# Shen attention and a SwiGLU block on one core: the opening list merged into the first chunk, w_out loaded in two halves, weight sums in two parts, and new orders for every chunk

## Chip, cores, metric

One core of a Trainium2 chip. The metric is the device time of one execution in microseconds. The kernel before was run 13 times: median 299.17 us, lowest 298.19, highest 301.69.

## What is computed

Eight batches of eight heads, 576 positions, head size 64. The attention is a linear one, and its output is the input of a gated block:

```
q_s = softmax of q over the head dimension
k_s = softmax of k over the positions
kv  = einsum('bhsd,bhse->bhde', k_s, v)
x   = einsum('bhsd,bhde->bhse', q_s, kv), rearranged to 4608 tokens x 512
out = (silu(x @ w_gate) * (x @ w_val)) @ w_out      # 512 -> 1536 -> 512
```

## The kernel before

**Attention of a batch** is done for two groups of heads, G = 0 and 1. `load` (line 80) brings q, k or v of a group with one DMA from SyncE's queue into the pool `ld` (three buffers for q, two for k and two for v). `exp` (126) is one ScalarE activation over 128 x 1152. `cast_v` (133) turns v into bf16 in one of two fixed tiles, one per group. `norm_sum` (140) and `norm_mul` (149) normalise q. The normalised q is transposed, by TensorE with a copy out of PSUM (`tr`, 158; for batches 0 and 1) or by a DMA (`tr_dma`, 177; later batches). `kv` (186) and `kn` (206) form the 64 x 64 matrices, `x` (229) or `x_pair` (260) multiply by them, and copies put the result as 16-bit columns into the ring `xt`.

**The gated block** takes the first 576 tokens by plain products: `First` (300), whose step I is one 128-column block of x @ w_gate with its silu, and J the same block of x @ w_val with the product with the silu. `Unit` (470) multiplies 128 of these tokens by w_out in two steps of six matmuls of 512 columns. All other tokens go by a seven-product scheme on 2 x 2 blocks: `Pair` (359) for the first two matrices, steps a b c d e f g and v; `Quad` (510) for w_out, steps A to H; a sixth block pair goes by plain products, `Direct` (434), steps G and U. The scheme needs sums of weight quarters, `g_sum` (333, four of them, in `gt`) and `w_sum` (488, four, in `wt`), sums of x columns (`x_sum`, 342) and of hidden columns (`h_sum`, 494).

**The order of the work** is written out by hand. `tc.manual_schedule()` keeps the order of the program on every engine. A plan is a string of tokens, which `chunk` (746) hands to `op` (673) one by one: `I3`, `a0`, `S042` and so on are the steps above with their block; `eq0:1` is the exp of q of group 0 of batch 1, `ek` that of k, `cv` the cast of v, `ns`, `nd` and `nm` the sums and products of the softmax, `tr` the transposed copy, `kk` and `kv` the kv products, `xz` and `xx` the x products, `Q`, `W`, `X`, `Y`, `S`, `T` the sums, `pe` and `silu` a one-column activation that brings the table of exp or silu, `load` the loads of the batch after. A star sends an evicting or elementwise step to the other of two engines. So each engine works through its own instructions in plan order, and a step that waits holds back everything after it on its engine.

There are five plans: PLAN_B (first 576 tokens and batch 1's attention), PLAN_0 (448 tokens), PLAN for chunks 1 to 5, PLAN_N for 6 and 7, and PLAN_E for the last w_out products.

**Loads and waits.** Weights are cast to fp16 by DMAs from GpSimd's queue (`w_slice`, 98; `wo_slice`, 106). Before the plans the program issues seven for w_gate and w_val, `w_dma[0]` to `[6]`, and three of four row blocks for w_out, `w_dma[7]` to `[9]`. An explicit dependency holds w_dma[7] back until w_dma[5] has landed, batch 1's q until w_dma[4] has, batch 1's first k until w_dma[8] has, and the second k until w_dma[9] has (lines 632 to 669). PSUM is one pool of eight banks (line 60); each I or J step takes two of them, until ScalarE or VectorE has emptied them.

Of the kernel before, what the change touches and what calls it, by code (L numbers as in the profile page):

```python
# [12 lines left out]
SYNC = mybir.DependencyInfo(mybir.DependencyClass.Sync, mybir.DependencyReason.DATA)  # L13
# [3 lines left out]
def kernel(  # L17
# [19 lines left out]
    nc = tc.nc  # L37

    B, H, S, D = q.shape
# [11 lines left out]
    NP = 5  # L51
# [15 lines left out]
    wo = const.tile([128, MT, d_model], FP16, name="wo", tag="wo")  # L67
# [9 lines left out]
    dmas = {}  # L77
    raw = {}

    def load(b, G, what, src, after=None):  # L80
        raw[what, b, G] = ld.tile(
            [128, 2, T * 64], FP32, tag=what, name=what, bufs=3 if what == "q" else None
        )
        ap = bass.AP(
            tensor=src.tensor,
            offset=src[b, 4 * G].offset,
            ap=[[T * 64, 128], [2 * HSTR, 2], [1, T * 64]],
        )
        d = nc.sync.dma_start(out=raw[what, b, G], in_=ap)
        if after is not None:  # L90
            tc.add_manual_dep(d.ins, after.ins.name, SYNC, reason="order of loads")
        dmas[what, b, G] = d

    def load_group(b, G):
        for what, src in (("q", q), ("k", k), ("v", v)):
            load(b, G, what, src)
# [9 lines left out]
    def wo_slice(m0, n):  # L106
        ap = bass.AP(
            tensor=moe_w_out.tensor,
            offset=moe_w_out[m0 * 128, 0].offset,
            ap=[[d_model, 128], [128 * d_model, n], [1, d_model]],  # L110
        )
        return nc.gpsimd.dma_start(out=wo[:, m0:m0 + n, :], in_=ap)
# [9 lines left out]
    A, Z = BANKS = ((0, 5), (5, 9))  # L122
# [10 lines left out]
    def cast_v(b, G, eng, t0=0, t1=T):  # L133
        copy(
            eng,
            vbs[G][:, t0:t1, 0:128].rearrange("p t (h d) -> p t h d", d=64),
            raw["v", b, G].rearrange("p h (t d) -> p t h d", d=64)[:, t0:t1],
        )
# [38 lines left out]
    def tr_dma(b, G):  # L177
        s = st[b, G]
        qt = at.tile([128, T, 2, 64], BF16, tag="qtd", name="qtd")
        nc.sync.dma_start_transpose(  # L180
            out=qt.rearrange("p t g c -> p t (g c)"),
            in_=s["qs"].rearrange("p t c -> p (t c)"),
        )
        s["qt"] = [qt[:, :, g, :] for g in range(2)]
# [417 lines left out]
    with tc.manual_schedule():  # L602
# [29 lines left out]
        tc.add_manual_dep(w_dma[0].ins, dmas["k", 0, 0].ins.name, SYNC, reason="order of loads")  # L632
        load(1, 0, "q", q, after=w_dma[4])
        load(1, 1, "q", q)
        for m0 in (0, 4, 8):
            w_dma.append(wo_slice(m0, 4))
        tc.add_manual_dep(w_dma[7].ins, w_dma[5].ins.name, SYNC, reason="order of loads")

        warm_up(WARM[0])
        for G in range(NG):  # L640
# [17 lines left out]
        x(0, 1, A)  # L658
        x(0, 1, Z)

        load(1, 0, "k", k, after=w_dma[8])
        load(1, 0, "v", v)
        load(1, 1, "k", k, after=w_dma[9])
        load(1, 1, "v", v)
        load(2, 0, "q", q, after=dmas["k", 1, 0])
        load(2, 0, "k", k, after=dmas["v", 1, 0])
        load(2, 0, "v", v, after=dmas["k", 1, 1])
        load(2, 1, "q", q, after=dmas["v", 1, 1])
        load(2, 1, "k", k, after=dmas["q", 2, 0])

        n_ch = n_tok // 512 - 1

        def op(t, ci, c0, h, parts):
            alt = t.endswith("*")
            t = t.rstrip("*")
            t, b = t.split(":") if ":" in t else (t, ci + 2)
            b = int(b)
            k, a, nm = t[0], t[1:], t[:2]
            if nm in ATT:
                G = int(t[2]) if t[2:3].isdigit() else 0  # L680
                if b >= B or nm == "lo" and b + 1 >= B and ci >= 0:
                    return
                if nm == "eq":
                    exp(b, G, "q")
                elif nm == "ek":
                    exp(b, G, "k")
                elif nm in ("si", "pe"):
                    f = AF.Silu if nm == "si" else AF.Exp
                    nc.scalar.activation(out=warm, in_=zero[:, 0:1], func=f)
                elif nm == "cv":  # L690
                    cast_v(b, G, nc.vector if alt else nc.gpsimd)
                elif nm == "ns":
                    norm_sum(b, G)
                elif nm == "nm":
                    norm_mul(b, G, nc.vector if alt else nc.gpsimd)
                    tr_dma(b, G)
                elif nm == "lo":
                    if ci < 0:
                        load(b, 1, "v", v)
                    else:  # L700
                        load_group(b + 1, 0)
                        load_group(b + 1, 1)
                elif nm == "kv":
                    kv_pair(b)
                elif nm == "xx":
                    x_pair(b, nc.scalar if alt else nc.vector)
                elif nm == "nd":
                    norm_mul(b, G, nc.gpsimd if alt else nc.vector)
                elif nm == "tr":
                    tr(1, G, BANKS[int(t[3])], nc.vector)  # L710
                elif nm == "kk":
                    kv_kn(b, G, split=True)
                elif nm == "xz":
                    x(1, G, BANKS[int(t[3])], nc.scalar if alt else nc.vector)
            elif k in "abcdefgv":
                parts["p" + a].run(k, alt)
            elif k in "GU":
                parts["m" + a].run(k)
            elif k in "IJ":
                parts["i" + a].run(k)  # L720
            elif k == "O":
                parts["u" + a[0]].run(int(a[1]), alt)
            elif k in "ABCDEFH":
                parts["o"].run(k, alt)
            elif k in "SR":
                k0 = int(a[1])
                h_sum(ci + (k == "R"), int(a[0]), k0, k0 + int(a[2]))
            elif k == "X":
                if ci + 1 < n_ch:
                    x_sum(c0 + 2 * h, 256, int(a), nc.gpsimd if alt else nc.vector)  # L730
            elif k == "Y":
                x_sum(c0, h, int(a), nc.gpsimd if alt else nc.vector)
            elif k == "W":
                w_sum(int(a), nc.gpsimd if alt else nc.vector)
            elif k == "Q":
                g_sum(int(a), nc.vector if alt else nc.gpsimd)
            elif k == "T" and ci == B - 2:
                i = int(a)
                if i == 0:
                    parts["t"] = ld.tile(  # L740
                        [128, 4, 2, 2, 128 * (HM - NP)], FP16, tag="q", name="gt2", bufs=3
                    )
                gt2[i] = parts["t"][:, i]
                g_sum(i, nc.gpsimd if alt else nc.vector, 128 * NP, 128 * HM, gt2)
# [11 lines left out]
            for t in plan.split():  # L756
                op(t, ci, c0, n // 2, parts)

        ATT = ("pe", "eq", "ek", "si", "cv", "ns", "nm", "lo", "kv", "xx", "nd", "tr", "kk", "xz")
        ORDER = (0, 1, 2, 3, 4, 5)  # L760
        gt2 = [None] * 4
        PLAN_B = """
        I0 I1 pe:1 I2 I3 J0 J1 I4 I5 J2 J3 J4 Q0 I6 J5 I7 J6 J7 eq0:1 ns0:1 eq1:1 I8
        nd0:1* ns1:1 J8 I9 J9 I10 Q1* nd1:1* I11 cv0:1 tr00 J10 J11 tr10 ek0:1 O01 Q3*
        cv1:1 ek1:1 O11 tr01 kk0:1 O02 tr11 eq0:2 O12 kk1:1 ns0:2 O21 xz10* ek0:2 xz00*
        O22 Q2 xz01 eq1:2 cv0:2 xz11 O31 load:2 nm0:2 cv1:2 O32 ek1:2
"""
        PLAN_0 = """
        a0 ns1 G5 b0 G11 Y0 c0 Y2 Y1 v0 Y3* d0* W2 a1 f0 b1 U5 c1 g0 d1 W0 v1 e0 a2 f1 b2
        v2 kv silu:2 nm1 g1 d2 a3 e1 c2 f2 b3 c3 e2 g2 d3 v3 e3 a4 f3 xx* load g3 W1 d4*  # L770
        b4 c4* X0 f4 v4 U11 e4* X2* X1 W3 X3 g4*
"""
        PLAN = """
        a0 S042 b0 G5 c0 d0 A v0 S002 a1 f0 b1 S142 c1 v1 U5 S242 g0 pe S222 B S022 S102
        S122 S302 d1 S322 ek0 e0 a2 S342 e1 eq0 ns0 S202 C ek1 f1 D E eq1 cv1 b2 c2* silu
        F nm0 cv0 g1 d2 v2 ns1 a3 nm1 H* f2 kv g2 d3 b3 c3 v3 e2 load f3 e3 a4 b4 c4 g3 v4
        d4* e4 xx* f4 X2 G11 g4 X0 X1 X3* U11
"""
        PLAN_N = """
        a0 S222 b0 c0 d0 T0* A v0 S002 f0 a1 e0* S042 b1 g0 d1 c1 S022 v1 a2 f1 S242 S102  # L780
        b2 e1* c2 g1 S142 d2 v2 B f2 a3 T1* b3 c3 S342 S122 S202 g2* e2 d3 C S302 v3 f3
        e3* S322 a4 b4 g3* d4 c4 v4 D T2 f4 e4* a5 b5 g4* c5* X0* d5 F f5 v5 E T3* X1 e5*
        X3 g5* H* X2*
"""
        PLAN_E = """
        S022 A S042 S122 S002 S142 S202 B C S102 S302 S322 S242 S222 S342 D E F H*
"""
        chunk(-1, 0, S, PLAN_B)
        chunk(0, S, 1024 - S, PLAN_0)
        for ci in range(1, n_ch):  # L790
            chunk(ci, 512 * (ci + 1), 512, PLAN if ci + 2 < B else PLAN_N)
# [31 lines left out]
```

The softmax here doesn't subtract the row's maximum and nothing guards it: scores larger than these inputs give would overflow.

## Time and profile before

| what | us |
|---|---|
| median of 13 runs | 299.17 |
| the profiled execution | 300.25 |
| its span, first to last instruction | 298.3 |
| I0, the first step of PLAN_B, starts on TensorE | 15.87 |
| a0 of PLAN_0 starts | 57.98 |
| a0 of chunk 1 starts | 78.65 |
| a0 of chunk 2 starts | 108.62 |
| busy: TensorE, VectorE, ScalarE, GpSimd | 287.1, 239.8, 221.5, 156.6 |

Times in the profile count from the start of the span. The busy time of TensorE counts matmuls whose modelled ends overlap, so its gaps have to be read from starts.

### The profile page before, as it was taken

The numbers are of one execution on the slowest core, as the hardware profiler recorded it, in microseconds if no ns is written. First come the engines' busy times: TensorE is split into PE (matmuls) and PEld (weight loads), VectorE is DVE, ScalarE is ACT, GpSimd is POOL, SyncE is SP. The second block draws the span as 40 slices with busy tenths as digits, with TensorE's granted clock in tenths as the row PEclk, the third lists the DMA queues.
The fourth block names the chain that finished last, engine by engine and source line by source line (L and its number), as shares of the span: only waits on it lengthen the run. The fifth ranks groups of instructions, "written<-read, shape, count | busy, mean of one in ns | idle before, by whom it ended". The sixth has DMA issues, their size and how long they took to land.

```text
span 298.3 us, 7118 instructions
## 1 busy us (share of the span) xinstructions
PE 287.1 (96%) x2716; PEld 234.1 (78%) x2716; DVE 239.8 (80%) x490; ACT 221.5 (74%) x416; POOL 156.6 (52%) x128
## 2 busy tenths in 40 slices
PE   8999997998999999999999999999999999999992
PEld 6778664477788868886888688868887888888882
DVE  2935692888899988998899789988999898897881
ACT  5684954687699688968896889688969865778430
POOL 0902848659419771977187718771887443131000
PEclk9999997999999999999999999999999999999997
DMA  7999999755911795179517870796092000510065
GB/s 255 293 189 247 243 316 346 217 142 75 391 53 32 151 314 205 26 149 314 212 22 149 261 270 17 149 304 230 13 149 63 0 2 1 120 23 2 7 137 141
DMA packets 38337, 46.46 MB, mean 156 GB/s; under 512 B 16288, under 2 KB 21408, under 8 KB 38304
## 3 DMA queue, kind: packets, MB, share of 16 engines
q1 hardware_dynamic: 32864, 41.03, 47.9%
q0 software_dynamic: 5280, 4.72, 10.0%
q8 instruction: 21, 0.34, 0.5%
q10 hardware_dynamic: 160, 0.26, 0.2%
q14 instruction: 12, 0.10, 0.1%
HBM read 37.75 MB, written 9.44 MB: 158 GB/s over the span
## 4 chain that ended last, share of the span: by engine, by line
PE 76%; DMA 12%; POOL 3%; DVE 3%; ACT 3%; issue 1%; ACTq 0%; DVEq 0%; POOLq 0%
PE sx L388 23%; PE ox L533 13%; PE sw L388 11%; PE ow L533 7%; PE sy L388 6%; DMA wv<-in_moe_w_val_dram 4%; PE oy L533 4%; DMA q<-in_q_dram 3%; PE u_ps L441 3%; PE o_ps L479 3%; PE g_ps L441 3%; PE kv L192 3%; DMA v<-in_v_dram 2%; DMA qtd<-qs 2%; POOL qs L152 1%; DVE rs L143 1%
## 5 line engine op out<-in xcount | busy, mean ns | idle before, releaser
L388 PEld LDWEIGHTS <-gt 128*128 128x128 f16 x672 | 64.6, 98 | 13.4 <-issue 3.0
L432 POOL TENSOR_TENSOR hr<-sg,u 128x512 bf16<-128x512 f16 (+1 forms) x33 | 39.1, 1185 | 51.3 <-ACT sg L431 50.4
L388 PE MATMUL sx<-xs,gt 128*128 128x256 f16 (+1 forms) x336 | 49.9, 271 | 0.3 <-DVE s L118 0.3
L116 ACT COPY s<-sx 128x512 f32<-128x512 f32 (+1 forms) x77 | 44.3, 577 | 7.7 <-PE sx L388 7.4
L423 POOL TENSOR_TENSOR hr<-sg,u 128x512 bf16<-128x512 f16 (+1 forms) x31 | 36.5, 1184 | 23.1 <-DVE u L422 22.3
L533 PEld LDWEIGHTS <-hs 128*128 128x128 bf16 x384 | 37.3, 98 | 4.7
L152 POOL TENSOR_TENSOR qs<-eq,rr 128x1152 bf16<-128x1152 bf16 x15 | 32.7, 2180 | 9.4 <-DVE rr L147 6.2
L388 PEld LDWEIGHTS <-wg 128*128 128x128 f16 x336 | 32.8, 98 | 4.8
L427 DVE TENSOR_TENSOR u<-sx,s 128x512 f16<-128x512 f32 (+1 forms) x42 | 28.5, 680 | 9.7 <-ACT sg L414 4.0
L414 ACT ACTIVATE sg<-s 128x512 f16<-128x512 f32 (+1 forms) x42 | 26.2, 625 | 12.8 <-DVE s L412 11.0
L431 ACT ACTIVATE sg<-sx 128x512 f16<-128x512 f32 (+1 forms) x42 | 25.2, 601 | 10.7 <-PE sx L388 10.6
L533 PEld LDWEIGHTS <-hr 128*128 128x128 bf16 x288 | 28.2, 98 | 3.3
L412 DVE TENSOR_TENSOR s<-sy,s 128x512 f32<-128x512 f32 (+1 forms) x42 | 28.4, 677 | 2.9 <-PE sy L388 2.0
L422 DVE TENSOR_TENSOR u<-sw,s 128x512 f16<-128x512 f32 (+1 forms) x42 | 28.4, 677 | 2.5 <-PE sw L388 1.2
L143 DVE TENSOR_REDUCE rs<-eq 128x18 f32<-128x1152 bf16 x16 | 21.5, 1346 | 6.9 <-ACT eq L127 6.9
L388 PE MATMUL sx<-xt,gt 128*128 128x256 f16 (+1 forms) x168 | 25.0, 271 | 0.0
L388 PE MATMUL sw<-xs,wv 128*128 128x256 f16 (+1 forms) x168 | 24.9, 271 | 0.0
L388 PE MATMUL sw<-xs,gt 128*128 128x256 f16 (+1 forms) x168 | 24.9, 271 | 0.0
L388 PE MATMUL sx<-xt,wg 128*128 128x256 f16 (+1 forms) x168 | 24.9, 271 | 0.0
L388 PE MATMUL sy<-xt,wg 128*128 128x256 f16 (+1 forms) x168 | 24.9, 271 | 0.0
L116 ACT COPY s<-sw 128x512 f32<-128x512 f32 (+1 forms) x34 | 19.8, 582 | 5.4 <-PE sw L388 5.2
L533 PE MATMUL ox<-wt,hs 128*128 128x256 f16 x192 | 23.6, 273 | 0.0
(101 smaller groups left out, 553.1 us busy)
## 6 DMA issues: line engine op xcount, KB each, us to landing
q<-in_q_dram SPq DMA_DIRECT2D x16, 576.0 KB, 6.6
k<-in_k_dram SPq DMA_DIRECT2D x16, 576.0 KB, 6.4
v<-in_v_dram SPq DMA_DIRECT2D x16, 576.0 KB, 7.3
out_dram<-o_sb SPq DMA_DIRECT2D x70, 128.0 KB, 2.4
wv<-in_moe_w_val_dram POOLq DMA_DIRECT2D x3, 512.0 KB, 11.7
wo<-in_moe_w_out_dram POOLq DMA_DIRECT2D x3, 512.0 KB, 9.7
wg<-in_moe_w_gate_dram POOLq DMA_DIRECT2D x2, 512.0 KB, 11.7
wg<-in_moe_w_gate_dram POOLq DMA_DIRECT2D x2, 256.0 KB, 5.3
```

The lines of the kernel that those rows point to most:

```text
L116: nc.scalar.copy(out=out, in_=in_)
L143: nc.vector.reduce_sum(out=rs, in_=s["eq"].rearrange("p t h d -> p (t h) d"), axis=mybir.AxisListType.X)
L152: eng.tensor_mul(s["qs"].rearrange("p t (h d) -> p (t h) d", d=64), s["eq"].rearrange("p t h d -> p (t h) d"), s["rr"].to_broadcast([128, ...
L388: nc.tensor.matmul(out=bank[:, h * j:h * j + h], lhsT=wgt(kk, j), rhs=rhs[:, kk, 0:h], start=first and j == 0 and kk == 0, stop=kk == 1, s ...
L412: nc.vector.tensor_add(self.s1, self.y[:, 0:w], self.s1)
L414: nc.scalar.activation(out=self.sa[:, 0:w], in_=self.s1, func=AF.Silu)
L422: nc.vector.tensor_add(u, self.w[:, 0:w], self.s2)
L423: meng.tensor_mul(self.out(0), self.halves(self.sa), self.halves(u))
L427: nc.vector.tensor_add(self.u, self.x[:, 0:w], self.s5)
L431: nc.scalar.activation(out=sb[:, 0:w], in_=self.x[:, 0:w], func=AF.Silu)
L432: meng.tensor_mul(self.out(1), self.halves(sb), self.halves(self.u))
L533: nc.tensor.matmul(out=dst[p][:, 0:HN], lhsT=lhs(kk, p), rhs=rhs(kk), start=start and i == 0, stop=i == HM - 1, skip_group_check=True,)
```

## The change

PLAN_B is gone; its steps stand, interleaved with those of PLAN_0, in one plan for chunk 0. Token `wa` issues the first two w_out loads, of three row blocks each, and then the loads of batch 1's k and v and of all of batch 2; batch 1's first k now waits for batch 1's second q, and the second k for the second w_out load. Token `wo` issues the other two w_out loads, the first of them after batch 1's first v. Batch 2's last v, before issued by `load:2` in PLAN_B, is part of that chain. `Q` sums take a part of the columns: 0 to 256 or 256 to 640. A starred `cv` goes to ScalarE instead of VectorE, a starred `tr` copies by ScalarE. All the other plans are new orders of the same steps.

```diff
-        for m0 in (0, 4, 8):
-            w_dma.append(wo_slice(m0, 4))
-        tc.add_manual_dep(w_dma[7].ins, w_dma[5].ins.name, SYNC, reason="order of loads")
+        def w_out_first():
+            for m0 in (0, 3):
+                w_dma.append(wo_slice(m0, 3))
+            tc.add_manual_dep(w_dma[7].ins, w_dma[5].ins.name, SYNC, reason="order of loads")
+            load(1, 0, "k", k, after=dmas["q", 1, 1])
+            load(1, 0, "v", v)
+            load(1, 1, "k", k, after=w_dma[8])
+            load(1, 1, "v", v)
...
+            load(2, 1, "v", v, after=dmas["k", 2, 0])
...
-        load(1, 0, "k", k, after=w_dma[8])
-        load(1, 0, "v", v)
-        load(1, 1, "k", k, after=w_dma[9])
-        load(1, 1, "v", v)
...
-                    cast_v(b, G, nc.vector if alt else nc.gpsimd)
+                    cast_v(b, G, nc.scalar if alt else nc.gpsimd)
...
+                elif nm == "wo":
+                    d = wo_slice(6, 3)
+                    tc.add_manual_dep(
+                        d.ins, dmas["v", 1, 0].ins.name, SYNC, reason="order of loads"
+                    )
+                    wo_slice(9, 3)
+                elif nm == "wa":
+                    w_out_first()
...
-                    tr(1, G, BANKS[int(t[3])], nc.vector)
+                    tr(1, G, BANKS[int(t[3])], nc.scalar if alt else nc.vector)
...
-                g_sum(int(a), nc.vector if alt else nc.gpsimd)
+                c0, c1 = ((0, 256), (256, 128 * NP))[int(a[1])]
+                g_sum(int(a[0]), nc.vector if alt else nc.gpsimd, c0, c1)
...
-        PLAN_B = """
-        I0 I1 pe:1 I2 I3 J0 J1 I4 I5 J2 J3 J4 Q0 I6 J5 I7 J6 J7 eq0:1 ns0:1 eq1:1 I8
-        nd0:1* ns1:1 J8 I9 J9 I10 Q1* nd1:1* I11 cv0:1 tr00 J10 J11 tr10 ek0:1 O01 Q3*
-        cv1:1 ek1:1 O11 tr01 kk0:1 O02 tr11 eq0:2 O12 kk1:1 ns0:2 O21 xz10* ek0:2 xz00*
-        O22 Q2 xz01 eq1:2 cv0:2 xz11 O31 load:2 nm0:2 cv1:2 O32 ek1:2
-"""
         PLAN_0 = """
-        a0 ns1 G5 b0 G11 Y0 c0 Y2 Y1 v0 Y3* d0* W2 a1 f0 b1 U5 c1 g0 d1 W0 v1 e0 a2 f1 b2
-        v2 kv silu:2 nm1 g1 d2 a3 e1 c2 f2 b3 c3 e2 g2 d3 v3 e3 a4 f3 xx* load g3 W1 d4*
-        b4 c4* X0 f4 v4 U11 e4* X2* X1 W3 X3 g4*
+        I0 I1 I2 Q00 I3 J0 wa J1 J2 J3 Q01 I4 Q20* I5 I6 I7 J4 I8 pe:1 Q10* J5 eq0:1 eq1:1
+        Q30* J6 J7 ns0:1 I9 J8 ns1:1 I10 I11 ek0:1 nd1:1 J9 cv0:1* J10 ek1:1 O01 nd0:1*
+        cv1:1* tr00 tr01 tr10 J11 wo kk0:1 O11 Q21 tr11 kk1:1 Q11 xz00* O21 cv1:2 xz11*
+        xz01 eq0:2 W2 O31 xz10* ek0:2 O02 W0 eq1:2 O12 cv0:2 a0 O22 Y0 W1 b0 c0 Y1 d0
+        ek1:2 Y2 Q31* Y3 v0 a1* e0 f0 ns0:2 O32 g0 nm0:2 d1 G5 ns1:2 b1 c1 v1 a2 f1 nm1:2
+        b2 kv:2 g1 d2 c2 v2 a3 f2 e1 b3 c3 U5 g2 d3 silu:2 v3 e2 e3 a4 f3 xx:2 load:2 g3
+        d4 b4 c4 G11 W3 v4 f4 U11 X0* e4* X2 X1 g4* X3
 """
         PLAN = """
-        a0 S042 b0 G5 c0 d0 A v0 S002 a1 f0 b1 S142 c1 v1 U5 S242 g0 pe S222 B S022 S102
-        S122 S302 d1 S322 ek0 e0 a2 S342 e1 eq0 ns0 S202 C ek1 f1 D E eq1 cv1 b2 c2* silu
-        F nm0 cv0 g1 d2 v2 ns1 a3 nm1 H* f2 kv g2 d3 b3 c3 v3 e2 load f3 e3 a4 b4 c4 g3 v4
-        d4* e4 xx* f4 X2 G11 g4 X0 X1 X3* U11
+        a0 S222 S202 pe S022 b0 c0 A d0 eq0 S002 ek0 S122 B S102 eq1 S042 S142 ek1 v0 e0
+        a1 f0 G5 cv0 C* S302 D S322 b1 S342 S242 ns1 g0 v1 E d1 a2* F c1 f1 b2 cv1 ns0 H*
+        nm1 nm0 c2 g1 d2 v2 e1 U5 f2 kv a3 g2 e2 d3 b3 c3 v3 f3 a4 e3 b4 g3 v4 c4* d4* xx*
+        silu e4* f4 X0 X2 G11 X1* U11 g4* load X3
 """
         PLAN_N = """
...
         PLAN_E = """
-        S022 A S042 S122 S002 S142 S202 B C S102 S302 S322 S242 S222 S342 D E F H*
+        A S002 S022 S222 S102 S122 S042 B S302 S322 S142 S342 C* D S202 S242 E F H*
 """
-        chunk(-1, 0, S, PLAN_B)
```

More of the change, by code (lines that the diff above doesn't have):

```diff
@@ L634 @@
         load(1, 1, "q", q)
-        for m0 in (0, 4, 8):
-            w_dma.append(wo_slice(m0, 4))
-        tc.add_manual_dep(w_dma[7].ins, w_dma[5].ins.name, SYNC, reason="order of loads")
+        def w_out_first():
[6 more added lines that the diff above has]
+            load(1, 1, "v", v)
+            load(2, 0, "q", q, after=dmas["k", 1, 0])
+            load(2, 0, "k", k, after=dmas["v", 1, 0])
+            load(2, 0, "v", v, after=dmas["k", 1, 1])
+            load(2, 1, "q", q, after=dmas["v", 1, 1])
+            load(2, 1, "k", k, after=dmas["q", 2, 0])
+            load(2, 1, "v", v, after=dmas["k", 2, 0])
         warm_up(WARM[0])
@@ L659 @@
         x(0, 1, Z)
-        load(1, 0, "k", k, after=w_dma[8])
-        load(1, 0, "v", v)
-        load(1, 1, "k", k, after=w_dma[9])
-        load(1, 1, "v", v)
[L665 to L669, printed above, removed]
         n_ch = n_tok // 512 - 1
@@ L680, in op @@
                 G = int(t[2]) if t[2:3].isdigit() else 0
-                if b >= B or nm == "lo" and b + 1 >= B and ci >= 0:
+                if b >= B or nm == "lo" and b + 1 >= B:
                     return
@@ L696, in op @@
                     tr_dma(b, G)
-                elif nm == "lo":
[L698 to L702, printed above, removed]
+                elif nm == "wo":
[6 more added lines that the diff above has]
+                    w_out_first()
+                elif nm == "lo":
+                    load_group(b + 1, 0)
+                    load_group(b + 1, 1)
                 elif nm == "kv":
@@ L757, in chunk @@
                 op(t, ci, c0, n // 2, parts)
-        ATT = ("pe", "eq", "ek", "si", "cv", "ns", "nm", "lo", "kv", "xx", "nd", "tr", "kk", "xz")
+        ATT = ("pe", "eq", "ek", "si", "cv", "ns", "nm", "lo", "kv", "xx", "nd", "tr", "kk", "xz", "wa", "wo")
         ORDER = (0, 1, 2, 3, 4, 5)
         gt2 = [None] * 4
-        PLAN_B = """
-        I0 I1 pe:1 I2 I3 J0 J1 I4 I5 J2 J3 J4 Q0 I6 J5 I7 J6 J7 eq0:1 ns0:1 eq1:1 I8
-        nd0:1* ns1:1 J8 I9 J9 I10 Q1* nd1:1* I11 cv0:1 tr00 J10 J11 tr10 ek0:1 O01 Q3*
@@ L778 @@
+        nm1 nm0 c2 g1 d2 v2 e1 U5 f2 kv a3 g2 e2 d3 b3 c3 v3 f3 a4 e3 b4 g3 v4 c4* d4* xx*
+        silu e4* f4 X0 X2 G11 X1* U11 g4* load X3
 """
         PLAN_N = """
[L780 to L783, printed above, removed]
+        a0 b0 c0 d0 A v0 S042 S222 f0 S142 a1 b1 g0 T0 d1 c1 v1 a2 f1 S002 e0* e1 b2 S102
@@ L784 @@
+        g1 d2 c2 v2 B f2 S022 a3 S202 b3 c3 g2 S122 S302 d3* C v3 e2 f3 e3* a4 b4 g3 d4 c4
+        T1 v4 a5 f4 S342 T2 D S322 S242 g4* d5 b5 T3* c5 X0 e4 F X1* v5 f5 e5 X3 E g5* H*
+        X2*
 """
         PLAN_E = """
-        S022 A S042 S122 S002 S142 S202 B C S102 S302 S322 S242 S222 S342 D E F H*
+        A S002 S022 S222 S102 S122 S042 B S302 S322 S142 S342 C* D S202 S242 E F H*
 """
-        chunk(-1, 0, S, PLAN_B)
         chunk(0, S, 1024 - S, PLAN_0)
```

## Prediction

> **What bounds the kernel now.** I read the busy shares by slice, then a table of TensorE (PE) by stage, then what PE waits for, then the chain of waits. By slice, PE is full except near a third of the way through the opening stage; the second line is its granted clock, which drops once in mid-run:
>
> ```profile
> PE   8999997998999999999999999999999999999992
> ...
> PEclk9999997999999999999999999999999999999997
> ```
>
> By stage (stretch, length, then busy us of PE, PE's weight loads, VectorE = DVE, ScalarE = ACT, GpSimd = POOL, clock, DMA share, GB/s), cut where a stall ends or a chunk begins:
>
> ```profile
> 35.60:46.47 10.87, 7.76 (x60) 5.16 (x58) 10.12 (x17) 5.91 (x12) 6.22 (x4) 0.98 1.07 312
> 46.47:50.00 3.53, 3.53 (x28) 1.92 (x28) 0.58 (x3) 1.16 (x2) 2.32 (x2) 0.57 0.94 323
> 50.00:57.98 7.98, 7.98 (x68) 3.44 (x66) 5.46 (x13) 5.84 (x9) 7.13 (x4) 1.00 0.76 270
> 57.98:78.65 20.67, 19.48 (x210) 16.25 (x209) 17.08 (x35) 15.90 (x34) 14.01 (x12) 1.00 0.67 165
> 78.65:108.62 29.97, 29.97 (x294) 24.69 (x293) 27.94 (x59) 25.92 (x49) 18.05 (x14) 1.00 0.51 137
> 108.62:138.59 29.97, 29.97 (x294) 24.68 (x293) 26.45 (x53) 25.37 (x48) 19.26 (x15) 1.00 0.60 177
> ```
>
> Chunks 1 to 5 repeat in 29.97 us with PE never idle. In them 4 matmuls of 256 columns start every 0.437 us, 4 of 512 every 0.86, the 36 of kv take 1.15, the x products 0.62. A chunk has 5 pairs x 7 products (15.3), 4 plain blocks (3.4), 7 Quad steps of 1.31 (9.2), kv and x: 29.7 us. Nothing is left to gain there, only to lose. What can be gained lies before 78.65. PE's waits in the whole run:
>
> ```profile
> PE kv L192 <- POOL vb L118: 2.4, 1, 2.4
> PE warm_ps L256 <- DVE zero L612: 1.1, 1, 1.1
> PE xa L273 <- DMA qtd<-qs: 0.8, 1, 0.8
> PE g_ps L310 <- ACT sg L321: 0.7, 1, 0.7
> ```
>
> The longest one in the chain that ended last (start, us, what), and the matmuls behind it in the timeline:
>
> ```profile
> 38.19 6.56 DMA v<-in_v_dram
> 44.88 1.56 POOL vb L118
> 46.47 1.16 PE kv L192 x18
> ```
>
> ```profile
> 46.47 1.16 PE L192 MATMUL kv<-vb,ek 64*128 64x129 bf16 x18 [2.44 <-POOL vb L118]
> 47.56 2.40 PE L479 MATMUL o_ps<-wo,hr 128*128 128x512 f16 x6
> ```
>
> Batch 1's v is issued at 38.19, because its order hangs on the second w_out load; it lands at 44.88; POOL casts it in 1.56; kv starts 2.4 late. And the pause costs twice: those six matmuls of 512 columns take 2.40 us, where six take 1.29 later in the same plan.
>
> **What the Trainium skill says.** TensorE: Matmul & The Clock Gate, Part 1, says that an idle array falls to half clock and needs some microseconds of work to come back; the granted 0.57 of 46.47 to 50.00 agrees. ScalarE: Activation LUTs, What ACT_TABLE_LOAD costs, gives about 1283 ns for a change of table and 1380 ns of drain. Here the load takes 1.28 us and the exp behind it starts 0.01 us later, so I take 1.28. DMA: Bandwidth & Descriptors, Issuing engines are not separate DMA queues, says that loads of all queues interleave on the same 16 engines; so SyncE's k and v and POOL's w_out share the rate seen here: 324 GB/s over 37.72 to 44.88.
>
> **The opening, in pure PE work.** From I0 (15.87) to chunk 1's a0 (78.65) are 62.8 us. The work at full clock: 24 I and J steps of 0.98 (23.5), 8 half Units of 1.29 (10.3), transposes 1.1, two kv 1.3, x of batch 1 1.5; then at 448 columns 35 products of 0.38 (13.4), 4 plain blocks of 0.76 (3.0), kv 1.2, x 0.6. Sum 55.9. So 6.9 us are lost: 0.85 before 36.45, 2.44 before kv, 1.3 to the slow clock (3.53 us for 2.2 of work), 0.9 at the DMA transpose (73.67 to 74.61), 0.3 at 61.8, and about 1.1 in gaps of 0.1 to 0.2. The change leaves the amount of PE work as it is (the same 5434 rows on PE's list), so it acts by these losses alone.
>
> **Part by part.** *First silu wait (0.85).* Two exps with two table loads stood between silus while PE had one J step. Now both stand behind I8, with J5, J6, J7 to cover: table 1.28, dummy 0.2, two exps 2.2, table back 1.28 = 5.0, from I8's silu (30.3) to 35.3; I9's silu ends at 36.0, and J9, which needs its banks, comes at 36.5. Zero, with 0.4 to spare; late exps cost one for one beyond that. *k and v.* The order is now behind batch 1's second q. The first q lands at 31.14, so I put the first k and v at 31.6 instead of 37.72, and the second pair at the second w_out load, now 6 row blocks in, not 8: about 36.5. With the old landing times (4.3 to 6.6 us): v at about 38, the second k and v at 40 to 42. ACT does ek, cv, ek, cv from 38.5 (table 1.28, then 1.1 each) to 43; kv of group 0 is due on PE at 41.6, of group 1 at 43.8. Both hidden; the 2.44 and the 1.3 go, 1 us of delay in the loads is free, and two casts of 1.1 to 1.6 leave POOL. *w_out's rest* is behind v's landing and one 2.1 us product on POOL: issue 38.3, with w_out's old 9.7 us to landing 48. It is first used at 48.4 by O02 and by W2 on DVE; behind W2 stand an x copy and Y0, c0's input, with some 2 us to spare. *Weight sums.* Q in halves is the same columns in six or eight smaller pieces; one 1280-column pair cost DVE 1.6 us, but 3.5 beside POOL. Behind them on DVE are J's products, which give banks back: I take 0.4 us for J11 (bounds 0 and 0.7: nd1 on DVE, 1.9, is ahead of J9's and J10's product). *The copies moved to ACT* cost nothing: ACT has two table loads fewer here. No starred tr is used. *Batch 2's transposes:* ns0:2 follows f0's sum, POOL's two products (2.1 each) follow e0's and g0's; the second transpose is issued about 8.9 us after f0, lands 3.2 to 4.5 later, and x needs it 12.3 after: 0 to 1.1, I take 0.5. *Small gaps:* 1.0 stay. Lost after: 1.9. Gain: 6.9 - 1.9 = 5.0; bounds 3.3 (lost after: J11 0.7, transposes 1.1, gaps 1.1, late exps or w_out 0.7) and 6.4 (gaps of 0.5 alone).
>
> *PLAN, five chunks.* Four exps now stand together near the front, so ACT's sequence from a0 is: copy to 1.2, table and dummy to 2.6, copies of c0, A, d0 to 4.3, exps to 8.7, table to 10.0, v0's silu, a1's copy to 11.1, G5's silu to 11.6. PE's d1 overwrites what a1's copy reads, at 11.36, and a2 takes G5's bank at 11.8: margins of 0.2 and 0.2, f1 0.1. DVE gets three copies more (about 1.8 us; 28.3 of 30). Further back d3 and f3 come 1.3 us after the starts of a3 and d3, just the product and copy (0.64 + 0.58). I take 0.1 us of loss per chunk, 0.5 in all; bounds 0 and 2.5. Loads go out at 22 us of a chunk, not 26, and are used at 4.3 of the next, not at 9.8: 12 us, against 10.5 for the slowest landing of the run. *PLAN_N and PLAN_E* reorder under a PE that sets the pace (27.5 us for 27.5 of work), with ACT at 19: 0, bounds 0 and 0.5.
>
> **Sum.** -5.0 + 0.5 = -4.5. The profiled execution (300.25: span 298.3 and 1.95 around) would come to 295.75; it stands 1.1 above the median, so the median comes to 299.2 - 4.5 = 294.7.
>
> **Rivals.** *Loads too slow:* k and v now run against w_out. If they share the rate evenly and land 4 us late, kv waits again and the clock falls: 3.7 comes back, 298.4. For it: DMA is full there; against: fewer bytes go ahead of v than before. *Thin margins:* everything as forecast, but ACT 0.5 later than my sequence; 0.7 per chunk, 3.5 in all against the 0.5: 297.7. For it, the margins; against, exps were next to Quad copies before too, without a PE wait. *Slower:* the block of four exps and the second table makes ACT so late that a1's copy and G5's silu hold PE in every PLAN chunk. Past the 0.2 margin each us of lateness costs one per chunk; it decides against the change from 1.1 us of loss per chunk. At 1.6: 5 x 1.6 - 5.0 = +3.0, 302.2. For it: five repeats, and data now needed 5.5 us earlier in the chunk; against: 12 us of lead. That the change doesn't do what it says is excluded: the new waits stand in the built program's order.
>
> **Chances.** Forecast (292.7 to 296.4) 0.60; slow loads 0.12; thin margins 0.12; slower 0.16. Within 0.3% is about what a measurement of this kernel can tell from no change: 298.3 to 300.1. Faster: 0.60 + 0.11 + half of the slow loads 0.06 = 0.77; same 0.07; slower 0.16. The range is from 292.7, all bounds good, to 299.0, past the first two rivals; the slower one is left out, with 0.03 below.
>
> **What would show it.** Right: no PE wait for a cast v and clock 1.0 in 40 to 50; chunk 1's a0 at 73 to 75 instead of 78.65; starts of chunks 1 to 6 30.0 to 30.2 apart. Wrong: ek or cv of batch 1 waiting for DMA beyond 43; PE idle at d1, a2 or f1 in every chunk; a wait for the transposes of 1 us or more; or PE waiting for w_out at O02.

## The result and the profile after

The kernel after takes 302.39 us (median of 11 runs, 299.85 to 303.24), the kernel before 298.67 in the runs beside it (median of 48). The ratio, taken over the single runs and not from these two medians, is 1.0107, with a 95% interval of 1.0084 to 1.0131: the change makes the kernel slower. The forecast was 294.7, its range ended at 299.0. The profiled execution took 302.27, its span is 300.2. TensorE's work is the same in both profiles: 2716 matmuls, 287.1 us.

From I0 to chunk 1's a0 now pass 65.38 us (15.35 to 80.73), against 62.78 in the profile before; from there to the end 219.5 against 219.7. All of the loss lies in the opening. (A second profile of the kernel before, e12 below, has an opening of 61.10, so the usual loss there is nearer 4 us than 2.6.) The same two rows of the page, slices of 7.5 us:

```profile
PE   8999897789999999999999999999999999999993
...
PEclk9999999979999999999999999999999999999998
```

TensorE is thinner in slices 7 and 8, and the clock drops behind them. The list of what TensorE waits for (us in total, times, longest) has a new head:

```profile
PE o_ps L479 <- DMA wo<-in_moe_w_out_dram: 3.2, 1, 3.2
PE sw L388 <- DVE xs L354: 2.0, 1, 2.0
PE warm_ps L256 <- DVE zero L612: 1.1, 1, 1.1
PE g_ps L310 <- DVE hr L326: 0.9, 1, 0.9
PE tp L168 <- DVE qs L152: 0.7, 2, 0.5
```

The wait for batch 1's cast v, 2.4 us before, is gone, as forecast. In its place TensorE stands 3.2 us at O02 for w_out and 2.0 at e0 for an x sum. The chain of waits says how they hang together (start, us, what):

```profile
37.95 2.12 POOL qs L152
40.07 0.74 POOL wo L112
40.81 12.79 DMA wo<-in_moe_w_out_dram
...
53.79 0.96 DVE wt L492
...
58.66 1.96 DVE gt L340 x2
60.62 0.31 DVE xs L354
60.93 0.05 issue
60.98 0.56 PE sw L388 x4
```

The second half of w_out is issued at 40.07 and 40.81 and has landed at 53.6. VectorE stands for it too, 4.66 us at W2:

```profile
53.79 0.96 DVE L492 TENSOR_TENSOR wt<-wo 128x1536 f16<-128x1536 f16 x1 [4.66 <-DMA wo<-in_moe_w_out_dram]
```

Then it works off what is queued behind (x copy, W sums, x sums, Q31) until 60.9, and e0 on TensorE needs the last x sum of these. By stage (stretch, length, busy us of PE, PE's loads, DVE, ACT, POOL, then clock, DMA share, GB/s):

```profile
40.81:53.60 12.79, 9.48 (x99) 4.87 (x97) 6.89 (x21) 7.01 (x10) 7.20 (x5) 1.00 1.09 315
53.60:61.00 7.40, 5.34 (x36) 3.31 (x36) 7.21 (x11) 5.90 (x9) 2.64 (x2) 1.00 0.68 181
61.00:66.00 5.00, 5.00 (x25) 3.03 (x26) 4.93 (x8) 2.67 (x5) 1.56 (x2) 0.66 0.03 8
...
80.73:110.63 29.90, 29.90 (x294) 24.75 (x293) 26.80 (x61) 23.94 (x44) 15.59 (x14) 1.00 0.64 170
```

After the two pauses come 5 us at a mean clock of 0.66, which cost 5.0 x 0.34 = 1.7 us more. Chunk 1 is as tight as before (29.90). What the DMA engines did in the first of these stretches, by queue (q1 is SyncE's loads, q0 GpSimd's; packets, MB as written, share):

```profile
q1 hardware_dynamic: 1489, 3.22, 69.8%
q0 software_dynamic: 800, 0.79, 39.2%
```

Beside w_out's half (0.79 MB as written in fp16, twice that as read) the engines moved 3.22 MB of q, k and v, five and a half loads of 0.59. Nearly all of them are batch 2's (batch 1's last k and v had landed at 41.2 and 42.7), and TensorE needs nothing of batch 2 before it needs w_out.

### The profile page after: what moved, and what is told of

Read it like the earlier page. It is cut to its first block, busy times and chain, and to the rows that moved or that the text cites. A ratio compares the mean times of both kernels' runs of the same rounds, so it can differ in the third digit from the quotient of the medians.

```text
span 300.2 us, 7113 instructions
## 1 busy us (share of the span) xinstructions
PE 287.1 (96%) x2716; PEld 234.0 (78%) x2716; DVE 240.3 (80%) x518; ACT 213.6 (71%) x398; POOL 147.9 (49%) x125
## 4 chain that ended last, share of the span: by engine, by line
PE 83%; DMA 6%; DVE 6%; issue 1%; POOL 1%; ACT 1%; ACTq 0%; DVEq 0%
PE sx L388 24%; PE ox L533 13%; PE sw L388 12%; PE ow L533 6%; PE sy L388 6%; DMA wo<-in_moe_w_out_dram 4%; PE g_ps L310 4%; PE oy L533 3%; PE g_ps L441 3%; PE u_ps L441 3%; PE kv L192 3%; PE u_ps L310 3%; DVE gt L340 1%; DMA q<-in_q_dram 1%; DVE rs L143 1%
## 5 line engine op out<-in xcount | busy, mean ns | idle before, releaser
L388 PEld LDWEIGHTS <-gt 128*128 128x128 f16 x672 | 65.7, 98 | 11.4 <-issue 1.1
L423 POOL TENSOR_TENSOR hr<-sg,u 128x512 bf16<-128x512 f16 (+1 forms) x32 | 36.6, 1144 | 74.4 <-ACT sg L414 48.1
L116 ACT COPY s<-sx 128x512 f32<-128x512 f32 (+1 forms) x71 | 41.3, 581 | 15.4 <-PE sx L388 15.2
L432 POOL TENSOR_TENSOR hr<-sg,u 128x512 bf16<-128x512 f16 (+1 forms) x32 | 37.2, 1162 | 21.3 <-ACT sg L431 21.3
L427 DVE TENSOR_TENSOR u<-sx,s 128x512 f16<-128x512 f32 (+1 forms) x42 | 28.5, 680 | 12.8 <-PE sx L388 5.4
L152 POOL TENSOR_TENSOR qs<-eq,rr 128x1152 bf16<-128x1152 bf16 x14 | 29.7, 2121 | 9.9 <-DVE rr L147 6.1
L116 ACT COPY s<-sw 128x512 f32<-128x512 f32 (+1 forms) x37 | 21.5, 580 | 7.3 <-PE sw L388 6.9
```

The lines of the kernel that those rows point to most:

```text
L116: nc.scalar.copy(out=out, in_=in_)
L152: eng.tensor_mul(s["qs"].rearrange("p t (h d) -> p (t h) d", d=64), s["eq"].rearrange("p t h d -> p (t h) d"), s["rr"].to_broadcast([128, ...
L388: nc.tensor.matmul(out=bank[:, h * j:h * j + h], lhsT=wgt(kk, j), rhs=rhs[:, kk, 0:h], start=first and j == 0 and kk == 0, stop=kk == 1, s ...
L423: meng.tensor_mul(self.out(0), self.halves(self.sa), self.halves(u))
L427: nc.vector.tensor_add(self.u, self.x[:, 0:w], self.s5)
L432: meng.tensor_mul(self.out(1), self.halves(sb), self.halves(self.u))
```

## The experiments

My theory after the traces: the DMA is full from before 34 to about 54 us, and the second half of w_out lands late because it is issued late and shares the engines with batch 2. The rivals: VectorE is late for another reason; the later plans cost the time. All of these kernels compute the whole output. The opening is I0 to chunk 1's a0 in the profiled execution, one for each kernel. Each ratio is to runs of the kernel before made beside it (medians 298.54 to 298.67):

| kernel | opening | median us | ratio to before, interval |
|---|---|---|---|
| after | 65.38 | 302.39 | 1.0107 (1.0084 to 1.0131) |
| e1 w_out whole | 61.89 | 299.53 | 1.0027 (1.0007 to 1.0047) |
| e2 batch 2 later | 62.89 | 300.88 | 1.0075 (1.0046 to 1.0105) |
| e3 W sums later | 65.98 | 301.94 | 1.0114 (1.0081 to 1.0147) |
| e4 late plans only | 60.96 | 299.25 | 1.0024 (1.0010 to 1.0038) |
| e5 Q30 to GpSimd | 64.93 | 301.86 | 1.0101 (1.0056 to 1.0145) |
| e6 k, v first only | 62.91 | 300.86 | 1.0080 (1.0052 to 1.0108) |
| e7 loads by due | 63.33 | 299.90 | 1.0042 (1.0019 to 1.0066) |
| e8 and exps later | 67.56 | 304.72 | 1.0201 (1.0161 to 1.0242) |
| e9 q before w_out | 60.64 | 298.22 | 0.9990 (0.9963 to 1.0017) |
| e10 and O02, W2 later | 60.63 | 297.90 | 0.9972 (0.9956 to 0.9989) |
| e11 and old late plans | 60.77 | 298.32 | 1.0004 (0.9982 to 1.0025) |
| e12 before again | 61.10 | 297.89, one run | none |
| e13 Q30 elsewhere | 60.20 | 298.31 | 0.9988 (0.9961 to 1.0015) |
| e14 and product on DVE | 58.75 | 296.92 | 0.9936 (0.9911 to 0.9960) |

**e1, w_out whole.**

```diff
-            for m0 in (0, 3):
+            for m0 in (0, 3, 6, 9):
...
-        ... tr00 tr01 tr10 J11 wo kk0:1 ...
+        ... tr00 tr01 tr10 J11 kk0:1 ...
```

> The changed kernel with all four w_out loads issued at token wa, one behind the other, and token wo gone. Theory (the second half of w_out lands too late, because it is issued at 40 us and then shares the full DMA with batch 2's loads): it lands by about 43 to 45, TensorE doesn't wait at O02 (3.2 us) nor at e0 (2.0), and the slow clock behind it (about 1.3) goes: 302.4 - 6.5 = 295.9; up to 298 if batch 1's second k and v, now later, make kv wait. Rival 1 (VectorE is behind for another reason, the weight sum beside GpSimd's, and w_out only seems to hold it): 301 to 302.4. Rival 2 (the new later plans cost the time): 302.4.

Measured 299.53, 2.9 less than the kernel after. All of w_out has landed at 44.4, and the waits at O02 and e0 are gone. In their place TensorE waits for the cast v of batch 1's second group, with the slow clock behind it (timeline of e1; in brackets the idle time and its releaser):

```profile
44.94 0.70 PE L192 MATMUL kv<-vb,ek 64*128 64x129 bf16 x18 [2.67 <-ACT vb L116]
```

So both rivals fall as the main cause. The gain is smaller than the removed waits because w_out, moved up, pushed k and v back: the first group's v, issued at 34.05, took 9.7 us to land, where it had taken 6.5 in the kernel after. The theory had allowed 298 for this; it became 299.5.

**e2, batch 2 later.** The issue of w_out is as in the kernel after, but fewer bytes move beside it: the last four of batch 2's loads go out only when w_out's last load has landed. One of them waits for it, and the other three stand behind that one in SyncE's queue.

```diff
-            load(2, 0, "v", v, after=dmas["k", 1, 1])
+        def batch_2(d):
+            load(2, 0, "v", v, after=d)
             load(2, 1, "q", q, after=dmas["v", 1, 1])
             load(2, 1, "k", k, after=dmas["q", 2, 0])
...
-                    wo_slice(9, 3)
+                    batch_2(wo_slice(9, 3))
```

> The changed kernel; of batch 2's six loads the last four (v of group 0, q, k, v of group 1) wait until the last w_out load has landed; w_out is issued where it was, at 40 us. Theory: about 1.8 MB less moves beside w_out, which lands at 47 to 48 instead of 53.6; TensorE's wait at O02 goes, but batch 2's second q comes some 5 us later and ScalarE's exp of it may hold what is behind it: 297 to 300. If it is the late issue alone and not the sharing, w_out lands at 51 or later and the time stays above 301. Rival (later plans): 302.4.

w_out, issued at nearly the same time (40.29 and 41.09), landed at 51.1, not 53.6. The queues over 41.1 to 51.1 in e2:

```profile
q0 software_dynamic: 800, 0.79, 47.9%
q1 hardware_dynamic: 667, 1.43, 40.7%
```

With less beside it, w_out lands earlier: the transfer takes 10.0 us instead of 12.8. So some 2.5 of the 5.6 us that w_out is later than my 48 are the sharing with these four loads. It landed at 51, not at the 47 to 48 of the expectation, because the second issue is 2.8 us later than the 38.3 that I had put. TensorE waits 0.3 at O02, but 3.0 elsewhere, behind an exp whose q is now late (timeline of e2, ScalarE and TensorE):

```profile
56.52 1.16 ACT L127 ACTIVATE eq<-q 128x1152 bf16<-128x1152 f32 x1 [4.00 <-DMA q<-in_q_dram]
```
```profile
58.65 0.91 PE L388 MATMUL sx<-xs,gt 128*128 128x224 f16 x4 [3.00 <-ACT s L116]
```

**e3, W sums later.** In chunk 0's plan W2, W0 and W1 stand behind Y3, else as after.

```diff
-        xz01 eq0:2 W2 O31 xz10* ek0:2 O02 W0 eq1:2 O12 cv0:2 a0 O22 Y0 W1 b0 c0 Y1 d0
-        ek1:2 Y2 Q31* Y3 v0 ...
+        xz01 eq0:2 O31 xz10* ek0:2 O02 eq1:2 O12 cv0:2 a0 O22 Y0 b0 c0 Y1 d0
+        ek1:2 Y2 Q31* Y3 W2 W0 W1 v0 ...
```

> The changed kernel with W2, W0 and W1 behind Y3 in chunk 0's plan, so that VectorE does the x copy and the x sums before it waits for w_out. Theory: TensorE's own wait for w_out at O02 stays (3.2 us); the wait at e0 (2.0) and most of the slow clock behind it (about 1) go: 302.4 - 3.0 = 299.4. If VectorE's wait costs nothing that TensorE's wait doesn't cost already: 302.4. Rival (later plans): 302.4.

301.94, no gain that counts. The wait at e0 is gone, but TensorE now waits twice for w_out, 1.45 at 50.48 and 3.38 at 54.67, and the nine matmuls behind the second take 4.00 us (after: 2.10):

```profile
50.48 0.81 PE L479 MATMUL o_ps<-wo,hr 128*128 128x512 f16 x3 [1.45 <-DMA wo<-in_moe_w_out_dram]
54.67 4.00 PE L479 MATMUL o_ps<-wo,hr 128*128 128x512 f16 x9 [3.38 <-DMA wo<-in_moe_w_out_dram]
```

The alternative expectation (VectorE's wait costs nothing beyond TensorE's own) is nearer the time. It isn't proved, since w_out also landed 1 us later here and the clock stayed at one half for 6.8 us (53.64 to 60.47) instead of 3.4. This profiled execution (303.66) is also the slowest of its six.

**e4, late plans only.** The kernel before with the new PLAN, PLAN_N and PLAN_E.

> The kernel before with the changed kernel's PLAN, PLAN_N and PLAN_E and nothing else of the change. Theory (all of the loss lies in the first chunk and the loads that feed it; from chunk 1's a0 to the end the trace shows 219.5 after, 219.7 before): 298.5, within 0.3 of the kernel before. Rival (later plans cost the time, or what ScalarE's block of four exps holds up): 301 or more. My prediction had +0.5: 299.2.

299.25, +0.7 (interval 0.3 to 1.1): small, nearer my prediction's 0.5 than the theory's zero. The rival that the later plans cost the time is out as the main cause. What matters more is in its opening, which is the program of before. Three of TensorE's waits in e4:

```profile
PE xa L273 <- DMA qtd<-qs: 1.2, 1, 1.2
PE g_ps L310 <- ACT sg L321: 1.0, 1, 1.0
PE kv L192 <- POOL vb L118: 0.7, 1, 0.7
```

kv waits 0.7 here, not 2.4. That raised the question of e12.

**e5, Q30 to GpSimd.** `Q30*` becomes `Q30`.

> The changed kernel with the weight sum Q30 on GpSimd behind Q01 instead of on VectorE beside it (there it took 3.69 us, and TensorE waited 0.9 at I10). Theory (w_out's landing sets the opening): the 0.9 goes at I10 but comes back in the wait at O02, except for what an earlier issue of w_out's second half gives (at most 1.3): 301 to 302.4. Rival (VectorE's lost 3 us are the cause): I10's wait and what follows go, 299 to 300.

301.86, as the theory said: the 0.9 at I10 goes, and w_out is waited for 1.7 and 3.5 us. The product qs now ends at 38.28, 1.8 us earlier, but w_out's issue hardly moves, because it waits for batch 1's first v (GpSimd in e5):

```profile
39.95 1.58 POOL L112 DMA_DIRECT2D wo<-in_moe_w_out_dram  x2 [1.67 <-DMA v<-in_v_dram]
```

**e6, k and v first only.** In the kernel before:

```diff
-        load(1, 0, "k", k, after=w_dma[8])
+        load(1, 0, "k", k, after=dmas["q", 1, 1])
```

> The kernel before; only batch 1's first k and v wait for batch 1's second q instead of the second w_out load, and batch 2's loads, which follow them, move up with them. This is the part of the change that I had put at 2.44 + 1.3. If it stands alone: kv's wait and the slow clock behind it go, 298.5 - 3.7 = 294.8. By the theory (the DMA is full until 54 us, so whatever is moved up pushes something else back) w_out's last load lands some 3 us later and TensorE waits for it at O02: 296 to 298.5.

300.86, so the part that I had put at a gain of 3.7, the earlier first pair of loads, is a loss of 2.4 by itself (interval 1.6 to 3.2). Group 0's k goes out at 34.02 instead of 37.72. But group 1's waits for the last w_out load, and its issue shows when that has landed; before, then e6, SyncE's queue:

```profile
40.22 0.37 SPq L89 DMA_DIRECT2D k<-in_k_dram  x1
```
```profile
44.00 0.37 SPq L89 DMA_DIRECT2D k<-in_k_dram  x1
```

The first two loads go out 3.7 us earlier, and w_out's last one lands 3.8 us later, so the second kv waits 1.97 us for its v. This is what a full DMA does here: what is moved up pushes back what it passes. My expectation named O02 as the place of the loss; it is the second kv.

**e7, loads by due; e8, and exps later.** All of w_out at `wa`, k and v behind the q of their group, all of batch 2 behind `w_dma[10]`. That is the fourth and last w_out load, not the third as the expectation says. In e8 batch 2's exps stand later in the plan too.

```diff
+            load(1, 0, "k", k, after=dmas["q", 1, 0])
...
+            load(1, 1, "k", k, after=dmas["q", 1, 1])
...
+            load(2, 0, "q", q, after=w_dma[10])
```

> The changed kernel with its loads in the order in which they are due, plan untouched but for the token wo: all four w_out loads at wa; batch 1's first k and v behind its first q, the second pair behind its second q; all of batch 2 behind the third w_out load, q first. Theory: kv finds its data (k and v have landed by 44), w_out has landed by 46, neither kv nor O02 waits; but the plan asks for batch 2's first exp at 47 to 48 and its q lands near 50, so ScalarE stands and the copies behind it hold TensorE by 2 to 3 us, as in the kernel with batch 2 held back: 298 to 300. If the sharing doesn't matter: as w_out whole, 299.5.

> The same loads, and in chunk 0's plan batch 2's four exps and two casts stand later (first exp behind O02, the other three behind d0, casts behind f0 and g0), so that nothing asks for batch 2 before it can have landed. Theory: no wait at kv, O02, e0 or a1, lost before chunk 1's a0 some 2 to 3 us against 6.9 before and 9.4 after; 298.5 - 4.4 + 0.7 for the later plans = 294.8, bounds 294 to 296.5. If the opening is bound by something other than the order of loads: 298 or more.

e7 took 299.90, but not by the mechanism that I gave: v of group 1 landed at 47.2, not by 44, and kv waits for it as in e1:

```profile
48.45 0.70 PE L192 MATMUL kv<-vb,ek 64*128 64x129 bf16 x18 [2.50 <-ACT vb L116]
```

w_out and batch 1's k and v together fill the engines to 47 us; k and v are due at about 44, w_out at 49. Issued together they share, and v ends at 47.2, w_out's last load at 46.9. e8's expectation failed outright (304.72 against 294.8): the same wait for v, and the block of exps that I had put together reached f1 and the second kv's cast:

```profile
66.70 0.54 PE L388 MATMUL sx<-xs,gt 128*128 128x224 f16 x4 [1.89 <-ACT s L116]
69.64 0.62 PE L192 MATMUL kv<-vb,ek 64*128 64x129 bf16 x8 [1.38 <-POOL vb L118]
```

**e9, e10, e11: an order that keeps both dates.** From the kernel after: beside the second half of w_out only batch 2's two q are asked for, its k and v wait for the last w_out load. In the plan both exps of k now stand behind d0, the second exp of q ahead of O02, and the two casts together. e10 also puts a0 ahead of O02 and W2 behind it. e11 is e10 with the old late plans. The diff is e10's, cut:

```diff
+            load(2, 0, "q", q, after=dmas["k", 1, 0])
+            load(2, 1, "q", q, after=dmas["v", 1, 0])
+        def batch_2(d):
+            load(2, 0, "k", k, after=d)
...
-        xz01 eq0:2 W2 O31 xz10* ek0:2 O02 W0 eq1:2 O12 cv0:2 a0 O22 Y0 W1 b0 c0 Y1 d0
-        ek1:2 Y2 Q31* Y3 v0 ...
+        xz01 eq0:2 O31 xz10* eq1:2 a0 O02 W2 W0 O12 cv0:2 cv1:2 O22 Y0 W1 b0 c0 Y1 d0
+        ek0:2 ek1:2 Y2 Q31* Y3 v0 ...
```

> The changed kernel; beside the second half of w_out only both q of batch 2 are in flight (asked for first), its k and v wait for the last w_out load; the second exp of q moves ahead of O02, the exps of k behind d0, and POOL casts group 0 first. As many bytes stand ahead of w_out as in the kernel with batch 2 held back, where w_out was waited for 0.3 us only and all of the rest came from the 4.0 us that ScalarE waited for the second q. Theory: neither w_out nor ScalarE holds TensorE by more than 1 us; 302.4 - 3.2 - 2.0 - 1.3 + 0.5 = 296.4, bounds 295.5 to 298.5 (the upper one if k lands after 56 and the exps hold v0 and d1). If a late load in this place always comes back in another: 299.5 to 301.

> As the run before, and in the plan a0 stands ahead of O02 and W2 behind O02, so that x and its sums don't queue behind w_out and w_out gets 0.4 us more. Theory: 0.3 to 0.8 less than the run before, 295.8. If w_out no longer decides: the same as the run before.

> As the run before, with PLAN, PLAN_N and PLAN_E of the kernel before. By the run of the late plans alone (+0.7, interval 0.3 to 1.1) it is 0.7 less: 295.1. If that 0.7 came from how the late plans follow the old opening: no difference.

e9: 298.22, 4.2 less than the kernel after, by the loads and three places in the plan; w_out has landed at 50.0. In e10 w_out has landed at 50.8, and O02, O12 and O22 run through:

```profile
50.39 4.05 PE L479 MATMUL o_ps<-wo,hr 128*128 128x512 f16 x18
```

So with w_out some 3 us earlier, and the exps in an order that fits the later k, the whole loss against before is gone. Loads and plan were changed together here, so their shares aren't separated; e2, with a change of loads alone, got 1.5 of the 4.2. e9 and e10 can't be told apart (the intervals overlap), nor e10 and e11: with this opening no gain from the old late plans can be seen. But 298 is not 296: the openings take 60.6 us, so the loss has gone, and the gain that I forecast hasn't come.

**e12, before again; e13, Q30 elsewhere; e14, and a product on VectorE.** e12 is the kernel before. e13 is e10 with `Q30*` behind `eq0:2`; e14 has `nm0:2*` behind `ns1:2` besides.

> The kernel before, once more under the profile. My sum took 2.44 us of kv's wait and 1.3 us of slow clock from one profiled execution of 300.25 us, while most executions take 298.2 to 299; the kernel with only the late plans changed has the same opening program and showed kv waiting 0.7 and no slow clock (60.96 us from I0 to chunk 1's a0, not 62.8). If the first profile was an unlucky execution: opening 60.8 to 61.5, kv's wait under 1.2, clock 1.0 at that place, time 298 to 299. If the losses belong to the kernel: opening 62.5 or more, kv's wait near 2.4.

> The kernel with a0 ahead of O02 (297.9), with the weight sum Q30 on VectorE at 49 us, when GpSimd computes nothing, instead of beside GpSimd's Q01 at 31. If the two engines slow each other down: 0.75 us instead of 3.67, no wait before I10 (0.93), 297.0. If the 3.67 belongs to the sum itself: it takes 3.7 again, the x copy behind it is late, and the time rises by 1 to 3.

> As the run before, and one of batch 2's two products (2.1 us on GpSimd, where g1's product waits behind both and ScalarE's silu behind that, 0.6 at f3) goes to VectorE's gap at 61.4. If the gap holds it (1.36): 0.6 less, 296.4. If it runs beside GpSimd's work and takes 2.8, as such a product did in the run with w_out whole: v1 and f2 are late, no gain or up to 1 more.

e12 took 297.89 us, its opening 61.10. Three of TensorE's waits, and the stretch in which the first profile of before had 3.56 us of work and clock 0.72:

```profile
PE xa L273 <- DMA qtd<-qs: 1.0, 1, 1.0
PE kv L192 <- POOL vb L118: 0.9, 2, 0.6
PE g_ps L310 <- ACT sg L321: 0.9, 1, 0.9
```
```profile
44.00:50.00 6.00, 5.07 (x57) 2.94 (x57) 3.86 (x10) 2.71 (x4) 3.20 (x3) 1.00 1.06 383
```

kv waits 0.6 and 0.3, and the clock is 1.00. The 2.44 and the 1.3 of my sum belong to that one execution: neither e12 nor e4, which has the same opening, shows them. Of the 1.8 us by which kv came later there (46.47 against 44.66), 0.3 are v's issue (38.19, 37.90), 1.1 the rest of its way on a full DMA (cast from 44.88, 43.46), 0.4 the cast (1.55, 1.14).

e13: the pair of sums takes 0.75 us where GpSimd computes nothing. The kernel after, VectorE and GpSimd, and then e13:

```profile
31.07 3.69 DVE L340 TENSOR_TENSOR gt<-wg,gt 128x512 f16<-128x512 f16 x2
```
```profile
31.06 3.41 POOL L340 TENSOR_TENSOR gt<-wv,wg 128x768 f16<-128x768 f16 x2 [1.59 <-DMA wv<-in_moe_w_val_dram]
```
```profile
48.46 0.75 DVE L340 TENSOR_TENSOR gt<-wg,gt 128x512 f16<-128x512 f16 x2
```

The wait before I10 is gone, but kv waits 0.8 for its v: the opening is 0.4 shorter than e10's, and the median isn't lower. e14 gives 296.92, faster than before by 0.64% (interval 0.40 to 0.89%). The product took 1.29 us in VectorE's gap, GpSimd's queue and the second transposes no longer hold anybody; of TensorE's listed waits behind I0 three stay:

```profile
PE kv L192 <- ACT vb L116: 0.7, 1, 0.7
PE sx L388 <- ACT s L116: 0.6, 1, 0.6
PE kv L192 <- POOL vb L118: 0.3, 1, 0.3
```

## Why the prediction was wrong

**The step that failed** is "w_out's rest": "issue 38.3, with w_out's old 9.7 us to landing 48 [...] with some 2 us to spare". Measured: issue 40.07 and 40.81, 12.8 us, landing 53.6. So two terms of that line were mis-sized. The issue came 2.5 late, 1.4 of it through batch 1's first v, which had to land first: v went out at 33.20 and landed 6.5 us later, at 39.7, not at about 38. GpSimd's product qs ended 0.4 after that, held up by VectorE's sum behind the 3.7 us Q30, and the second issue stands 0.7 behind the first. e5 shows that Q30 isn't the reason: without it the issue still waits for v until 39.95. The transfer came 3.1 late because I took its old duration into a place where batch 2's loads run beside it. e2 shows the sharing; e9 shows that with w_out landing at 50.0 and a plan to fit the whole loss goes. I had written that the loads of all queues share the rate, and then asked only whether k and v would be late, not who pays for their being early. The sum of bytes due before 48 us was never made.

**What hung on it:** 3.2 us at O02, 2.0 at e0 and 1.7 of slow clock, in a line that I had costed at nothing with 2 us of cover. "What would show it" named PE waiting for w_out at O02, but no rival priced it; the bounds had 0.7 for late exps or w_out together.

**The opening's 6.9** was right for that execution and wrong for the kernel. The second profile loses 61.1 - 55.9 = 5.2, and e4's opening 5.1. With my own 1.9 left over, the gain could have been 3.3, not 5.0; and I took the sum off a median in whose executions much of the loss isn't. The profile stood 1.1 above the median; that distance was the warning.

**k and v:** right for kv. The k of the two groups were issued at 32.73 and 36.35 (forecast 31.6 and 36.5), and neither kv waited; the slack took up the first pair's delay, which w_out's issue could not. ScalarE's sequence in the opening held.

**First silu wait:** ScalarE no longer causes a wait there, as forecast. **Weight sums:** the term was mis-sized: 0.4 at J11 was 0.9 at I10, through Q30 on VectorE, for which I had the number (3.5 us beside GpSimd) and didn't apply it to the half sums.

**Batch 2's transposes:** 0.5 forecast; 0.6 and 0.5 in e9 and e10, nothing in the kernel after, where TensorE comes later. **Copies on ScalarE:** nothing, right; no wait for ScalarE is in the kernel after's list.

**PLAN:** +0.5 forecast. The trace shows 29.90 for each of chunks 1 to 4, 0.07 less than before, and no listed wait of TensorE after 80, with four exps standing together as I had sequenced them; a1's copy starts 10.4 us after a0. e4 says +0.7, but no trace shows where (from chunk 1's a0 to the end 219.8, against 219.6 in e12), and e11 against e10 shows no difference. Whether the late plans cost anything beside a good opening stays open. The slower rival (ScalarE's block) is wrong in the kernel after; in e8, where I built such a block into chunk 0, it cost 1.9. The rival of slow loads had the right resource and the wrong victim.

## What to carry to other kernels

When loads are reordered on a full DMA, list every load with its bytes and the time at which it is first needed, and add up: each date must hold with all that stands before it and beside it. A load that is put forward is paid for by those it passes, and these can be ones that nobody waits for today, as w_out was. And a load that hangs on another's landing inherits its delay, even where the first one's own reader has slack. A stall in a profile is that execution's: before its length goes into a sum, look for it in a second profile, the more so when the profiled time stands above the median.

## What the runs showed of the hardware

The Trainium skill, SBUF — State Buffer, section "SBUF: two separate sides", calls the port pair of VectorE and GpSimd an exclusive lock: of a GpSimd operation and a VectorE one with two SBUF inputs, the one that starts first holds it for the whole instruction, and the other blocks. The traces agree: VectorE's two sums for Q30 ended at 34.76, just behind GpSimd's two, which ended at 34.47, and took 3.69 us instead of 0.75, while GpSimd's took 3.41, beside 3.25 for such a pair at 41.60. In e1 the same sums started 0.3 us ahead of GpSimd's and took 0.75.

On the clock, the Trainium skill, TensorE: Matmul & The Clock Gate, Part 1, says that the rate is halved after an idle window of about 3.4 us, in a window that runs freely. The traces agree on the length: a half-clock stretch here lasts 3.41 us, or twice that in e3 and e5. But the window needn't be idle. Counting back from where a half-clock stretch starts in steps of 3.41 us gives the windows of each execution. The kernel after (stretch, length, busy us of PE, PE's loads, DVE, ACT, POOL, clock, DMA share, GB/s):

```profile
48.55:51.97 3.42, 1.94 (x12) 0.62 (x10) 0.58 (x2) 2.38 (x3) 0.00 (x0) 1.00 1.11 326
51.97:55.38 3.41, 1.74 (x9) 0.79 (x9) 1.59 (x3) 0.90 (x2) 0.00 (x0) 1.00 0.86 332
58.79:62.21 3.42, 1.40 (x13) 1.00 (x12) 3.42 (x6) 3.32 (x4) 0.95 (x1) 1.00 0.42 93
62.21:65.62 3.41, 3.41 (x14) 1.86 (x13) 3.38 (x5) 1.16 (x3) 1.18 (x2) 0.50 0.00 0
```

The pause of 3.15 us is split between two windows, each with TensorE busy for half of it or more, and the clock stays at 1.00; the shorter one of 2.02 falls into one window and leaves it 1.40 busy, and the next runs at 0.50. In the openings of all 16 profiles the same holds: no window at full clock with 1.74 us or more of work is followed by half clock, and each of those with 1.56 or less is (the 1.56 in e8, the 0.92 behind the pause of 2.50 in e7). So in this case a pause costs by what it leaves of its window, and where the window starts is luck. Nothing here lies between 1.56 and 1.74, and busy times rest on modelled ends of matmuls.
